# Input products by blocks in chained banks from chunk 7 on, with the sums of w_in made earlier

## The chip, the cores and the metric

The kernel runs on one core of one Trainium2 chip. The metric is the device time of one execution in microseconds (us), the median of several runs. All times below are us unless they are marked ns. The engines are TensorE (PE; PEld is its weight load), VectorE (DVE), ScalarE (ACT), GpSimd (POOL) and SyncE (SP), which here issues the DMAs.

## The reference

Attention with random features for 8 batches, 8 heads, 576 positions and head size 64, followed by a gated feed-forward layer over all 4608 rows:

```python
q_s, k_s = q * scale, k * scale
def phi(x):
    h = x @ omega.T - sum(x * x) / 2
    return exp(h - max(h)) / sqrt(m)          # m = 128 features
kv, z = phi(k_s).T @ v, sum(phi(k_s))
x = (phi(q_s) @ kv) / (phi(q_s) @ z + 1e-6)   # per head; heads side by side: 4608 x 512
h = x @ w_in                                  # 512 x 2048
g = h * tanh(softplus(h))                     # Mish
out = g @ w_out                               # 2048 x 512
```

## The kernel before

The 4608 rows are cut into 18 chunks of 256 rows. For every chunk c the kernel makes the x of its two tiles of 128 rows (attention), an input stage (h = x w_in, Mish, g) and an output stage (g w_out). Operands of the large products are split into two float16 parts, high and low, and a product is three matmuls: low times high, high times low, high times high. The input stage of chunk c stands beside the output stage of chunk c-1: the string `order` in the main loop says for each chunk in what order an input step (`i`) and an output step (`o`) are written. One output step is 12 matmuls of 512 columns into `po`.

The attention runs ahead, as items: one for each batch and pair of heads of k, one for each row tile of q. `pace` says how many items have been given out by a point of a chunk. An item is a generator that runs through the steps of an agenda, one step sixteen times a chunk. An item splits its input (`sk`, `sq`: ScalarE the high part, GpSimd the low), makes the projections (`pk`, `pq`), takes the maximum and subtracts it on VectorE, takes the exponential on ScalarE (`ek`, `eq`), splits again (`kp`, `qn`), and makes `pkv` (keys times values), or transposes by DMA (`qp`) and makes `pn` (queries times `kv`). Values come in as `vf`, with a maximum per batch (`vmx`, then the scale `s_v`), and are split into `vb`. The x of a tile is split into `xs` and transposed by DMA into `xT`. A scheduler orders each engine's instructions from this writing, with costs of its own.

The input stage has two forms:

- `ff_in`, up to chunk 14, is the plain one. A step makes two of the 16 column tiles of h: 24 matmuls of 256 columns into a bank `ph` (pool `ps_h`, two banks). `later(1, mish, ...)` lets ScalarE take Mish out of the bank one step later, and `g_split` splits the result into `g` another step later.
- `ff_in7`, from chunk `SC0` = 15 on, multiplies 2 x 2 blocks by Winograd's scheme with seven products in place of eight. A step is one product: 24 matmuls of 128 columns. Half a chunk's columns (`gr` 0 or 1) takes seven steps. The left operands are blocks of w_in (a11, a12, a22) and four sums of blocks (s1 to s4); the right ones are blocks of x and sums of them (t1 to t4), which `x_sums` makes: four differences on VectorE, four splits and four transposes a chunk in place of two (regions 2 and 3 of x go to tiles `xm`). Each product has a bank `p_...` of its own in `ps_a` (four banks, shared with the attention), and VectorE adds the banks up in the tile `h` (L801).

The sums of w_in are made by `s_make`, in four pieces, written from 16 x (SC0 - 6) + 2 steps behind the start of chunk 2, that is in chunks 11 to 13. VectorE adds and splits, ScalarE copies, and the 16 results go to a scratch in DRAM (`ds`). `ask_sum` loads them back, 256 KB at a time, into a ring of three pairs of slots (`w`), one pair after each product that used a sum.

## Time and profile before

| | |
|---|---|
| median of 3 runs | 964.44 (963.3 to 964.82) |
| the profiled execution | 962.69 |
| its span | 960.8 |
| instructions | 20397 |
| granted TensorE clock, mean | 0.992 |
| busy: PE, PEld, DVE, ACT, POOL | 940.9, 679.3, 624.9, 633.9, 222.7 |
| DMA | 100.25 MB, 147403 packets |

The span runs from the first to the last instruction of one profiled execution; the profiled execution's own time is longer by what lies around the span. A busy time is the sum of an engine's instructions, of which each begins when its inputs are there, so a wait shows as the idle time before an instruction and not in the instruction itself. A matmul's end is modelled, so the length of a group of matmuls is best taken from one group's start to the next one's. A name such as `po<-wo,g` says what an instruction writes and reads, and an arrow behind an idle time names what ended it. "The chain that ended last" is followed back from the last instruction; what stands in it is what set the end.

### The profile page before, as it was taken

The page shows a single profiled execution, that of the slowest core. Times are in us where ns is not written, and L with a number is a line of the kernel's source. Part 1 is how long each engine was busy: PE and PEld are TensorE (multiplying, and loading weights), DVE is VectorE, ACT ScalarE, POOL GpSimd, SP SyncE. Part 2 cuts the span into 40 slices and gives each one's busy share as a digit, 9 for nine tenths or more (in the row PEclk, how much of TensorE's full clock was granted, in tenths as well). Part 3 has the DMA queues.
Part 4 walks back from the last instruction along what each step waited for, and adds up shares of the span by engine and source line. Part 5 has one row for each costly group of instructions (what it writes and reads, how often), then busy time and mean ns, then how long its engine had stood idle before and what let it go on. Part 6 is the DMA issues. An engine that isn't in the chain of part 4 may idle for free. (4 is left out here: it accounts for less than half of the span.)

```text
span 960.8 us, 20397 instructions
## 1 busy us (share of the span) xinstructions
PE 940.9 (98%) x8568; PEld 679.3 (71%) x8568; DVE 624.9 (65%) x1080; ACT 633.9 (66%) x818; POOL 222.7 (23%) x141
## 2 busy tenths in 40 slices
PE   9999988999999999999999999999989999999998
PEld 6788873677677777777777777777756777777663
DVE  5879797587766666656575655788889656643330
ACT  4758875686877877768667775778776866332231
POOL 0000052242432322322133333222231332200000
PEclk9979999999999999999999999999999999999999
DMA  9866314431741346313431253423552145634410
GB/s 287 271 208 208 109 48 94 102 58 61 140 92 37 107 77 119 69 59 75 101 68 53 69 118 66 93 89 68 136 124 73 37 100 115 172 117 131 133 57 33
DMA packets 147403, 100.25 MB, mean 104 GB/s; under 512 B 112112, under 2 KB 124528, under 8 KB 147312
## 3 DMA queue, kind: packets, MB, share of 16 engines
q1 hardware_dynamic: 147312, 98.95, 41.2%
q8 instruction: 67, 1.10, 0.5%
q14 instruction: 24, 0.20, 0.1%
HBM read 58.95 MB, written 13.63 MB: 76 GB/s over the span
## 5 line engine op out<-in xcount | busy, mean ns | idle before, releaser
L858 PE MATMUL po<-wo,g 128*128 128x512 f16 x1632 | 375.2, 380 | 0.0
L689 PE MATMUL ph<-xT,w 128*128 128x256 f16 (+1 forms) x2816 | 344.8, 279 | 0.7 <-ACT xT L72 0.7
L689 PEld LDWEIGHTS <-w 128*128 128x128 f16 x2688 | 261.0, 98 | 47.3 <-issue 0.7
L858 PEld LDWEIGHTS <-g 128*128 128x128 f16 x1632 | 155.1, 98 | 163.9 <-issue 2.2
L83 DVE SCALAR_TENSOR_TENSOR g<-h,us,g 128x1024 f16<-128x1024 f32 (+3 forms) x92 | 120.2, 1316 | 36.8 <-ACT g L72 36.2
L834 ACT ACTIVATE h<-ph,us 128x512 f32<-128x512 f32 (+3 forms) x152 | 83.3, 573 | 77.6 <-PE ph L689 76.8
L81 POOL TENSOR_TENSOR sq<-fq,sq 64x1024 f16<-64x1024 f32 x31 | 69.0, 2227 | 159.1 <-issue 65.2
L81 POOL TENSOR_TENSOR sk<-fk,sk 64x1152 f16<-64x1152 f32 x24 | 60.5, 2520 | 111.5 <-ACT sk L72 86.9
L81 POOL TENSOR_TENSOR xs<-x,xs 128x512 f16<-128x512 f32 (+1 forms) x35 | 44.2, 1264 | 151.9 <-issue 68.0
L72 ACT ACTIVATE g<-h,us 128x1024 f16<-128x1024 f32 (+3 forms) x80 | 72.6, 932 | 1.2
L834 ACT ACT_TABLE_LOAD x55 | 70.6, 1283 | 1.0
L364 ACT ACT_TABLE_LOAD x53 | 68.0, 1283 | 4.2 <-DVE ek L358 3.3
L349 DVE TENSOR_REDUCE mxq<-pq 128x4 f32<-128x512 f32 x72 | 46.8, 682 | 31.7 <-PE pq L340 31.6
L792 PEld LDWEIGHTS <-w 128*128 128x128 f16 x1008 | 58.4, 98 | 5.9
L81 DVE TENSOR_TENSOR qn<-eq,qn 128x1024 f16<-128x1024 f32 x31 | 38.9, 1254 | 36.2 <-ACT qn L72 36.2
L349 DVE TENSOR_REDUCE mxk<-pk 128x4 f32<-128x512 f32 (+1 forms) x96 | 50.1, 548 | 18.0 <-PE pk L340 18.0
L834 ACT ACTIVATE h<-h,us 128x1024 f32<-128x1024 f32 (+2 forms) x16 | 14.7, 933 | 61.9 <-DVE h L801 61.9
L72 ACT ACTIVATE o<-po,us 128x512 f32<-128x512 f32 (+1 forms) x38 | 25.8, 680 | 40.1 <-PE po L858 40.0
L81 DVE TENSOR_TENSOR kp<-ek,kp 128x1152 f16<-128x1152 f32 x24 | 36.4, 1515 | 24.0 <-ACT kp L72 24.0
L364 ACT ACTIVATE eq<-eq,lnt 128x1024 f32<-128x1024 f32 x31 | 35.6, 1148 | 21.2 <-DVE eq L358 21.0
L81 POOL TENSOR_TENSOR vb<-vf,vb 128x640 f16<-128x640 f32 x24 | 39.4, 1641 | 40.6 <-DVE vb L74 28.7
L801 DVE TENSOR_TENSOR h<-p_s,h 128x512 f32<-128x512 f32 x30 | 20.2, 689 | 43.2 <-PE p_s L792 43.2
(140 smaller groups left out, 1156.9 us busy)
## 6 DMA issues: line engine op xcount, KB each, us to landing
w<-ds SPq DMA_DIRECT2D x48, 256.0 KB, 3.4
vf<-in_vL_dram SPq DMA_DIRECT2D x32, 325.0 KB, 3.3
fq<-in_qT_dram SPq DMA_DIRECT2D x36, 256.0 KB, 3.6
out_dram<-o SPq DMA_DIRECT2D x36, 256.0 KB, 2.3
fk<-in_kT_dram SPq DMA_DIRECT2D x24, 256.0 KB, 3.6
raw<-in_w_out_dram SPq DMA_DIRECT2D x5, 1024.0 KB, 8.9
wo<-in_w_in_dram SPq DMA_DIRECT2D x4, 1024.0 KB, 13.2
raw<-in_w_in_dram SPq DMA_DIRECT2D x4, 1024.0 KB, 15.2
```

Of the source, the lines that this page charges most:

```text
L72: act.activation(out, in_, AF.Copy, scale=scale)
L81: eng.tensor_tensor(out=out, in0=in_, in1=hi, op=ALU.subtract)
L83: eng.scalar_tensor_tensor(out=out, in0=in_, scalar=scale, in1=hi, op0=ALU.mult, op1=ALU.subtract)
L349: sub = dve.tensor_reduce(out=mx[:, lo:hi], in_=pp[:, :m, :], axis=AX.X, op=ALU.max, negate=by_act)
L364: last = act.activation(e, e, AF.Exp, bias=lnt)
L689: nc.tensor.matmul(out=ph[:, i, :], lhsT=wi(a, k, f) if c else wi0(k, f), rhs=xT[c][:, y, k, :] if c else xT0()[:, k, :], start=n == 0, st ...
L792: nc.tensor.matmul(out=ph[:, i, :], lhsT=left(gr, op_l, i, a, k), rhs=x_region(c, r)[:, y, k0 + k, :], start=n == 0, stop=n == len(mm) - 1,)
L801: dve.tensor_tensor(out=out, in0=bank, in1=in0, op=ALU.add)
L834: act.activation(h[:, :, lo:hi], ph[:, :, lo:hi], AF.Mish, scale=us[:, 0:1])
L858: nc.tensor.matmul(out=po[i], lhsT=gT[c, gr][:, a, f % FG, i * P:(i + 1) * P], rhs=wo(y, f), start=f == 0 and (a, y) == parts[0], stop=f = ...
```

## The change

`SC0` goes from 15 to 7: chunks 7 to 14 get the block form too, and `s_make` is started at 16 x (7 - 6) + 2 steps behind the start of chunk 2, in chunks 3 to 6. In `ff_in7` the products of a half chunk are chained in banks. The bank `pa` (now of `ps_h`) takes a11, s2, s3 and a22 one on top of the other, and after a11, s2 and s3 ScalarE copies its state into a quarter of h (c11, c12, c22). `pd`, the other bank of `ps_h`, takes s1 and then s4, and VectorE adds it to c22 after s1 and s3 and to c12 after s4. `pb`, of `ps_a`, takes a12, and VectorE adds it to c11. The fourth quarter, c21, is never copied: `mish7` lets ScalarE take Mish straight from `pa`. VectorE makes three adds of 128x512 for a half chunk; ScalarE makes three copies.

The order of the steps is the same but for the last two of each half (`iio` in place of `ioi`), `SUMS` swaps s1 and s3, the tiles `xm` get tags of their own (2 and 1 buffers), the pool of h tiles has 4 buffers in place of 5, the tile `idle` of the first spinning matmuls becomes a part of a weight slot, and from chunk 2 on TensorE's instructions are kept in the order in which they are written (`manual_schedule`).

```diff
-    SC0 = 15
+    SC0 = 7
...
-    idle = const.tile([P, 512], F16, name="idle")
+    idle = slots[NB][:, 0, 0:512]
...
-            x_more[c, r] = sb.tile([P, 2, n, P], F16, tag="vf", name=f"xm{c}_{r}", bufs=5)
+            x_more[c, r] = sb.tile([P, 2, n, P], F16, tag=f"xm{r}", name=f"xm{c}_{r}", bufs=4 - r)
...
-    SUMS = ("s2", "s3", "s1", "s4")
+    SUMS = ("s2", "s1", "s3", "s4")
...
-        def products(gr, op_l, op_r):
+        def products(bank, gr, op_l, op_r, first):
...
-            ph = ps_a.tile([P, FQ, P], F32, tag="a", name=f"p_{op_l}_{c}_{gr}")
             for i in range(FQ):
                 for n, (a, y, k) in enumerate(mm):
                     nc.tensor.matmul(
-                        out=ph[:, i, :], lhsT=left(gr, op_l, i, a, k), rhs=x_region(c, r)[:, y, k0 + k, :],
-                        start=n == 0, stop=n == len(mm) - 1,
+                        out=bank[:, i, :], lhsT=left(gr, op_l, i, a, k), rhs=x_region(c, r)[:, y, k0 + k, :],
+                        start=first and i == 0 and n == 0, stop=n == len(mm) - 1, skip_group_check=True,
                     )
...
-            p1 = products(gr, "a11", "b11")
-            cast(act, c21, p1)
+            pa = bank(ps_h, "h", f"pa{c}_{gr}")
+            products(pa, gr, "a11", "b11", True)
+            cast(act, c11, pa)
             yield
-            add(c11, c21, products(gr, "a12", "b21"))
+            pb = bank(ps_a, "a", f"pb{c}_{gr}")
+            products(pb, gr, "a12", "b21", True)
+            add(c11, pb)
             yield
-            add(c12, c21, products(gr, "s2", "t2"))
+            products(pa, gr, "s2", "t2", False)
+            cast(act, c12, pa)
             yield
-            add(c21, c12, products(gr, "s3", "t3"))
+            pd = bank(ps_h, "h", f"pd{c}_{gr}")
+            products(pd, gr, "s1", "t1", True)
             yield
-            p5 = products(gr, "s1", "t1")
-            add(c22, c21, p5)
-            add(c12, c12, p5)
+            products(pa, gr, "s3", "t3", False)
+            cast(act, c22, pa)
+            add(c22, pd)
             yield
-            add(c12, c12, products(gr, "s4", "b22"))
+            products(pa, gr, "a22", "t4", False)
+            yield
+            products(pd, gr, "s4", "b22", False)
+            add(c12, pd)
+            later(0, mish7, sp, h[1], pa)
+            later(1, g_split, c, gr, 1, sp, h[1])
             later(1, mish, sp, h[0], h[0])
             later(2, g_split, c, gr, 0, sp, h[0])
             yield
-            add(c21, c21, products(gr, "a22", "t4"))
-            later(1, mish, sp, h[1], h[1])
-            later(2, g_split, c, gr, 1, sp, h[1])
-            yield
+
+    def mish7(sp, h, pa):
+
+        for us, lo, hi in sp:
+            if lo < P:
+                e = min(hi, P)
+                act.activation(h[:, :, lo:e], pa[:, :, lo:e], AF.Mish, scale=us[:, 0:1])
+            if hi > P:
+                b = max(lo, P)
+                act.activation(h[:, :, b:hi], h[:, :, b:hi], AF.Mish, scale=us[:, 0:1])
...
-    GB, HB, QB = 4, 5, 1
+    GB, HB, QB = 4, 4, 1
...
+    own = ExitStack()
+    own.enter_context(tc.manual_schedule(engines={mybir.EngineType.PE}))
     for c in range(2, NCH):
         fi, fo = (ff_in if c < SC0 else ff_in7)(c), ff_out(c - 1)
-        order = "io" * 8 if c < SC0 else "iioiioioioi" * 2
+        order = "io" * 8 if c < SC0 else "iioiioioiio" * 2
...
+    own.close()
```

Where the instructions come to stand is shown at three places near the start of chunk 8. First ScalarE before, from the end of chunk 7's second half on (`h` is the tile that takes Mish, `sk` a key item's high part, `eq` and `qn` of a query item):

```order
L834 ACT_TABLE_LOAD
L834 ACTIVATE h_1_1_5353<-ph_1_1_2_5429,us_4234 128x512
L72 ACTIVATE g_1_5195<-h_1_1_5353,us_4234 128x1024
L72 ACTIVATE o_1_5555<-po_1_4945,us_2920 64x512
L72 ACTIVATE o_1_5555<-po_1_4945,us_4234 64x512
L834 ACTIVATE h_0_0_5523<-ph_0_0_0_5524,us_4234 128x512
L834 ACTIVATE h_0_0_5523<-ph_0_0_2_5580,us_4234 128x512
L72 ACTIVATE g_0_5522<-h_0_0_5523,us_4234 128x1024
L72 ACTIVATE sk_1_5799<-fk_1_5714 64x1152
L364 ACT_TABLE_LOAD
L364 ACTIVATE eq_5633<-eq_5633,lnt 128x1024
L72 ACTIVATE qn_5709<-eq_5633 128x1024
```

Now, in the first half of chunk 8:

```order
L72 ACTIVATE h_0_0_5861<-pa_0_5863 128x4x128
L365 ACT_TABLE_LOAD
L365 ACTIVATE eq_5920<-eq_5920,lnt 128x1024
L72 ACTIVATE qn_6032<-eq_5920 128x1024
L72 ACTIVATE h_0_1_5862<-pa_0_5863 128x4x128
L72 ACTIVATE sk_2_6484<-fk_2_6280 64x1152
L847 ACT_TABLE_LOAD
L847 ACTIVATE h_0_1_5862<-h_0_1_5862,us_4364 128x4x128
L365 ACT_TABLE_LOAD
L365 ACTIVATE ek_0_6118<-ek_0_6118,lnt 128x1152
L844 ACT_TABLE_LOAD
L844 ACTIVATE h_0_1_5862<-pa_0_5863,us_4364 128x4x128
```

The first row is the copy to c12, the fifth the copy to c22, the last the Mish that frees `pa`. Between the two copies stand an exponential and a split, and between c22 and the freeing Mish another exponential with its table load.

Second, VectorE in the first half of chunk 8 before:

```order
L358 TENSOR_TENSOR ek_0_5758<-pk_0_0_5760,mxk_0_5759 128x512
L358 TENSOR_TENSOR ek_0_5758<-pk_0_4_5769,mxk_0_5759 128x128
L349 TENSOR_REDUCE mxk_0_5759<-pk_0_5_5772 128x4
L83 SCALAR_TENSOR_TENSOR g_0_5522<-h_0_1_5681,us_4234,g_0_5522 128x1024
L358 TENSOR_TENSOR ek_0_5758<-pk_0_5_5772,mxk_0_5759 128x512
```

Now:

```order
L350 TENSOR_REDUCE mxk_0_6119<-pk_0_0_6120 128x4
L803 TENSOR_TENSOR h_0_1_5862<-pd_0_6002,h_0_1_5862 128x4x128
L359 TENSOR_TENSOR ek_0_6118<-pk_0_0_6120,mxk_0_6119 128x512
L350 TENSOR_REDUCE mxk_0_6119<-pk_0_4_6129 128x1
L350 TENSOR_REDUCE mxk_0_6119<-pk_0_5_6132 128x4
L359 TENSOR_TENSOR ek_0_6118<-pk_0_4_6129,mxk_0_6119 128x128
L359 TENSOR_TENSOR ek_0_6118<-pk_0_5_6132,mxk_0_6119 128x512
L803 TENSOR_TENSOR h_0_0_5861<-pd_0_6002,h_0_0_5861 128x4x128
```

The adds of `pd` to c22 and to c12 (L803) now stand among the maxima and differences of a key item.

Third, SP around the same place, before and then now:

```order
L305 DMA fk_2_5865<-in_kT_dram 64x2x512
L305 DMA fk_2_5865<-in_kT_dram 64x2x64
L481 DMA_TRANSPOSE qp_5550<-qn_5485 128x16x128
L575 DMA_TRANSPOSE xT_4869<-xs_5515 128x8x128
L890 DMA out_dram<-o_1_5555 128x512
```

```order
L540 DMA_TRANSPOSE xm_3_4853<-xs_3_4784 128x4x128
L765 DMA w_81<-ds_0_0_2671 128x2x512
L765 DMA w_82<-ds_0_1_3153 128x2x512
L306 DMA fk_2_6280<-in_kT_dram 64x2x512
L306 DMA fk_2_6280<-in_kT_dram 64x2x64
L540 DMA_TRANSPOSE xT_5024<-xs_1_5851 128x8x128
L540 DMA_TRANSPOSE xm_2_5961<-xs_2_5916 128x8x128
L482 DMA_TRANSPOSE qp_5966<-qn_5855 128x16x128
```

Loads of the sums (`w<-ds`) and two more transposes of x stand ahead of the query transpose (`qp`).

## The prediction

> **What bounds the kernel now.** I read the busy shares first, then busy time chunk by chunk, then the chain that ended last, then the waits of ScalarE and the DMA landings.

> ```profile
> PE 940.9 (98%) x8568; PEld 679.3 (71%) x8568; DVE 624.9 (65%) x1080; ACT 633.9 (66%) x818; POOL 222.7 (23%) x141
> ```

> TensorE is busy for 98% of the span and nothing else passes 71%. A shift of TensorE work should move the end one for one, as long as TensorE does not wait. Next the stretches between the first matmuls of successive output stages; the rows are chunks 3, 4, 5, 6, 8, 12, 13 and 16. Columns: stretch, length, busy PE, PEld, DVE, ACT, POOL, granted clock, DMA share, GB/s.

> ```profile
> 227.98:277.56 49.58, 48.73 (x460) 34.95 (x457) 34.29 (x67) 39.46 (x44) 17.57 (x10) 1.00 0.54 112
> 277.56:326.76 49.20, 49.20 (x475) 35.67 (x473) 30.58 (x62) 38.87 (x52) 16.13 (x9) 1.00 0.22 54
> 326.76:375.46 48.70, 48.70 (x481) 34.98 (x479) 29.55 (x51) 35.65 (x38) 13.62 (x8) 1.00 0.54 99
> 375.46:424.56 49.10, 49.10 (x471) 35.60 (x469) 30.02 (x63) 38.68 (x50) 16.38 (x9) 1.00 0.31 65
> 472.33:521.33 49.00, 49.00 (x469) 35.51 (x467) 29.04 (x54) 30.16 (x31) 12.66 (x7) 1.00 0.26 60
> 667.97:719.93 51.96, 49.48 (x437) 34.29 (x435) 46.11 (x78) 38.77 (x43) 14.96 (x8) 0.97 0.56 126
> 719.93:771.02 51.09, 49.59 (x480) 35.84 (x478) 40.46 (x56) 38.79 (x56) 12.15 (x6) 1.00 0.18 56
> 859.79:899.27 39.48, 39.48 (x436) 28.14 (x433) 14.09 (x18) 11.37 (x13) 0.00 (x0) 1.00 0.38 121
> ```

> A plain chunk takes 49.0 with no idle TensorE. Chunk 16, which already uses the block products, takes 39.48, but has no attention work beside it. Chunks 12 and 13, which hold the sums of w_in, lose 2.48 and 1.50. The chain prices the pieces.

> ```profile
> 810.20 2.62 PE ph L689 x24
> 813.72 2.59 PE po L858 x12
> 882.29 2.68 PE p_s L792 x48
> 887.56 1.34 PE p_s L792 x24
> ```

> Half a plain pair (24 matmuls of 256 columns) is 2.62, one product 1.34, an output group 2.59. Check: 14 x 1.34 + 8 x 2.59 = 39.48, chunk 16 to the digit, so products cost nothing beyond their columns.

> **TensorE work removed.** Chunks 7 to 14 go from 8 x 2.62 = 20.96 to 14 x 1.34 = 18.76: 2.20 per chunk, 17.6 over eight. It is on the path throughout. The attention items are paced by chunk, so their matmuls per chunk stay.

> **Handed-out order of TensorE.** The instruction orders with and without it differ in one place of chunk 3, where two po matmuls stood between two pk groups. Cost 0, at most one pk group (0.7) either way; the rest of the change does not rest on it.

> **The other engines in chunks 7 to 14.**

> ```profile
> L801 DVE TENSOR_TENSOR h<-p_s,h x30: 677/691/692, 823.7 to 932.3; 128x512 f32<-128x512 f32 x30
> L72 ACT ACTIVATE h<-p_a x5: 577/577/597, 840.7 to 918.7; 128x512 f32<-128x512 f32 x5
> L561 DVE TENSOR_TENSOR tt<-x,x x3: 416/416/424, 785.0 to 831.3; 128x256 f32<-128x256 f32 x3
> L834 ACT ACTIVATE h<-ph,us x34: 369/687/690, 425.2 to 618.1; 128x512 f32<-128x512 f32 x32, 128x128 f32<-128x128 f32 x1, 128x384 f32<-128x384 f32 x1
> L764 SPq DMA_DIRECT2D w<-ds x48: 517/518/962, 632.5 to 923.1; - x48
> ```

> VectorE gains per chunk 6 adds (4.1), 4 differences of x (1.7) and about 0.7 of larger splits: 29.0 becomes 35.5 of 46.8, 76%. ScalarE gains 6 copies (3.5), loses about 0.9 of Mish (8 x 0.687 against four 128x512 and two whole tiles), and the order has 14 table loads fewer, 2.2 per chunk at the 1.28 shown below: nearly level. GpSimd gains about 2 for two more remainders of x. SP gains 16 loads (8.3 of issue) and 2 transposes. None becomes the bound by busy time. The smaller pool of h tiles (4 for 5) and the idle tile's new place cost nothing: a half chunk uses two h tiles, and the first writer of that slot comes after the spins. Bound: one wait of 0.7 (an add) either way.

> **The sums of w_in, chunks 3 to 6 instead of 11 to 13.** In the old place, the sums' own instructions (length, DVE, ACT, clock, DMA share, GB/s), TensorE's waits there (total, times, longest), and the output groups ahead of and behind the longest:

> ```profile
> 618.67:771.02 152.35, 48.13 (x55) 10.02 (x16) 0.99 0.34 86
> ...
> PE pk L340 <- DVE x L511: 2.4, 1, 2.4
> PE pkv L445 <- DVE kp L81: 1.9, 2, 1.5
> ...
> 698.32 2.75 PE L858 MATMUL po<-wo,g 128*128 128x512 f16 x12
> 707.08 4.44 PE L858 MATMUL po<-wo,g 128*128 128x512 f16 x12
> ```

> 48.1 of VectorE. It cost a wait of 2.4 and one of 1.5; behind the first, twelve po matmuls took 4.44 where the group ahead took 2.75, with a granted clock of 0.97 over that chunk: 1.7 more. Together 5.6. The new chunks hold 34.3, 30.6, 29.6 and 30.0 of VectorE; with 12 each they come to 42 to 46 of 49, the level of chunks 12 and 13. So I move the 5.6, net 0. Bounds: -5.6 (all hidden) to +5.6 (twice the waits).

> **The waits that the chain of banks adds.** This decides. A plain bank had to be emptied within po + ph + po, 7.8. Now pa takes five products with ScalarE reading between them: after a11 and after s2 the cover is 1.34 + 2.59 = 3.93, after s3 it is 2.59, and Mish must leave pa within s4 + po = 3.93 before the next a11. pd needs c22 from ScalarE, then VectorE's add, within 3.93. Attention matmuls add some 0.7 to each. A copy takes 0.58, so a start up to 2.0 late is free after s3, up to 3.35 elsewhere. How late ScalarE comes today, in its worst quiet place:

> ```profile
> 426.83 1.28 ACT L364 ACT_TABLE_LOAD   x1
> 428.11 2.78 PE L689 MATMUL ph<-xT,w 128*128 128x256 f16 x24
> 429.45 0.82 DVE L278 TENSOR_REDUCE vmx<-vf 128x1 f32<-128x640 f32 x1 [3.68 <-DMA vf<-in_vL_dram]
> 432.49 0.69 DVE L358 TENSOR_TENSOR ek<-pk,mxk 128x512 f32<-128x512 f32 x1
> 433.21 1.26 ACT L364 ACTIVATE ek<-ek,lnt 128x1152 f32<-128x1152 f32 x1 [5.10 <-DVE ek L358]
> 434.54 1.15 ACT L72 ACTIVATE kp<-ek 128x1152 f16<-128x1152 f32 x1
> 435.71 1.28 ACT L834 ACT_TABLE_LOAD   x1
> 437.00 0.69 ACT L834 ACTIVATE h<-ph,us 128x512 f32<-128x512 f32 x1
> ```

> ph ended at 428.11 + 2.78 = 430.89, its Mish began at 437.00, 6.1 late: VectorE stood before a V tile's maximum, ScalarE's exponential behind VectorE, the Mish behind both. TensorE felt nothing. How often, over 340 to 620 (5.7 chunks; total, times, longest):

> ```profile
> ACT h L834 <- PE ph L689: 48.0, 19, 4.5
> ACT ek L364 <- DVE ek L358: 8.9, 4, 5.1
> ACT eq L364 <- DVE eq L358: 5.9, 5, 2.1
> ACT vf L434 <- DVE s_v L124: 5.0, 2, 3.6
> ```

> In 19 cases ScalarE waits for TensorE, as wished. The five eq waits stay under the cover. The six others hold 13.9, and each keeps an exponential and a copy behind it (1.26 + 1.15): 6 x 2.41 = 14.5. Less six covers of 3.35: 8.3 per 5.7 chunks, 11.6 in eight. With the 0.7 of attention in each cover: 4.1, or 5.8 in eight. I take 9, between them. Bounds: 0 (chunk 16) and, with the cover of 2.0 each time, (28.4 - 12.0) x 8 / 5.7 = 23. Behind a product that waits stand, on TensorE, the next output group and the next attention group, and for these VectorE's maxima wait; such a wait empties the other queues too, so I add no second one. pb's place among ps_a's four banks and VectorE's larger share lie inside them.

> [...] Trace: kp ends at 435.69, the load starts at 435.71, Mish at 437.00, so a switch costs 1.28, and Mish leaves pa 1.28 + 0.69 after a22 at best, with 1.96 to spare. [...]

> **Loads and transposes.** Landing times, of qp (stretch 420 to 620) and of the sums (819 to 936):

> ```profile
> DMA to landing us min/median/max: 4.3/4.5/6.3
> ...
> w<-ds SPq DMA_DIRECT2D x42, 256.0 KB, 3.5
> ```

> A slot of the ring is asked for when its product ends and needed 9.2 later at the soonest (s2 to s4: three products and two output groups); two issues of 0.52 and 3.5 leave 4.7. A load that waits for its product holds SP, and the next key loads and qp transposes queue behind it; pn on TensorE waits for qp. Taken at 0, bound 1 per half chunk, 16.

> **Sum.** The profiled execution took 962.69, 1.85 outside its span. 962.69 - 17.6 + 0 + 9 = 954.1. The median of the runs shown, 964.44, is 1.75 above the profiled one: 955.8.

> **Rivals.**

> *The cover holds.* Waits under 4: 946.8 to 951, if the sums cost what they did. For it: the 19 waits of ScalarE for TensorE, and an order that puts most copies ahead of the exponentials. Chance 0.22.

> *Late weights or transposes.* SP waits for buffers that GpSimd frees, and a ring load behind such a wait is late; at 1 per half chunk, without the 9, 962.8. Against: 4.7 of slack. Chance 0.10.

> *Slower: ScalarE's lateness reaches TensorE whole, and the clock drops with it.* Place: a22 behind the copy to c22. A lateness of 6.1 costs 6.1 + 0.58 - 2.59 = 4.1 there, and 1.7 at the lower clock as behind the wait of 2.4: 5.8. More than three of them in eight chunks decide; one per chunk gives 964.4 - 17.6 + 46 = 993, five give 976. Against: such a lateness must meet the shortest cover. Chance 0.12. [...]

> *The sums hurt twice in chunks 3 to 6*: +5.6, 961.4. Chance 0.04.

> [...] The rows above speak against it; chance 0.02. [...]

> **Chances and range.** The forecast has 0.50, own range 951 to 960. Faster by over 0.2% (below 962.5; 0.2% is about what a measurement tells from no change): 0.49 + 0.22 + half of 0.10 + 0.03 = 0.79. Within: 0.08. Slower: 0.13. The range 946 to 967 leaves out the far end of the slower rival (0.11) and a little of the first (0.04).

> **What would show it.** Right: chunks 8 to 10 near 46.8 + 1.1 each, products of 1.34, waits of pa and pd on ACT and DVE of 1 to 4 adding up to about 9, waits of 4 to 6 in chunks 3 to 6 and none left at 706 and 742. Wrong: PE waits on w<-ds or qp, a granted clock under 0.98 in several of chunks 7 to 14, or chunks 7 to 14 at 49.

## The result and the profile after

The changed kernel takes 1006.62 us (median of 4 runs, 1002.34 to 1022.67) against 963.87 for the kernel before: a ratio of 1.042, 95% interval 1.039 to 1.046. It is 4% slower; forecast were 955.8, at most 967. The profiled execution took 1008.6, its span 1006.5.

In some executions, of the kernel before too, the whole takes about 20 us more (in the traces of such executions, `chain_sc15` for one, the granted clock is 0.51 from 15 to 57 us), so single times and medians of few runs below can hold these 20, and stretches are compared from the start of chunk 2 on, behind that time.

The busy shares of the kernel after:

```profile
PE 942.6 (94%) x9720; PEld 688.4 (68%) x9720; DVE 656.0 (65%) x1152; ACT 646.3 (64%) x844; POOL 238.4 (24%) x157
```

TensorE is now idle for 1006.5 - 942.6 = 63.9, before for 19.9: 44.0 more. And its busy time did not fall by the 17.6 of the removed columns; it grew by 1.7. The missing 19.3 are nearly all matmuls at half clock: a mean granted clock of 0.974 over 1006.5, against 0.992 over 960.8, is 18.5 us of lost clock more. So the 45.7 between the spans are 44.0 of idle time and 19.3 of slower matmuls, less the 17.6. No engine took over as the bound: VectorE stands at the same share as before, ScalarE two points lower.

By stretches, first of the kernel before, then after. The rows are chunk 2, chunks 3 to 6 (new place of the sums), 7 to 14 (new block products), and 15 to 17 (block products in both). Columns as in the prediction: length, busy PE, PEld, DVE, ACT, POOL, granted clock, DMA share, GB/s.

```profile
176.54:227.98 51.44, 51.13 (x519) 37.38 (x516) 37.37 (x64) 37.98 (x47) 18.26 (x10) 1.00 0.40 82
227.98:424.56 196.58, 195.73 (x1877) 141.19 (x1875) 124.44 (x240) 152.66 (x181) 63.70 (x36) 1.00 0.40 83
424.56:819.57 395.01, 390.61 (x3712) 280.20 (x3709) 275.10 (x459) 286.55 (x330) 112.09 (x64) 1.00 0.39 87
819.57:936.08 116.51, 116.51 (x1279) 82.54 (x1276) 48.17 (x77) 36.05 (x45) 4.52 (x4) 1.00 0.41 122
```

```profile
179.41:231.29 51.88, 51.13 (x518) 37.46 (x515) 40.20 (x66) 39.47 (x49) 18.29 (x10) 1.00 0.36 85
231.29:444.56 213.27, 201.41 (x1902) 143.57 (x1899) 175.39 (x306) 155.37 (x190) 68.58 (x40) 0.98 0.43 103
444.56:865.51 420.95, 384.92 (x4839) 285.21 (x4837) 265.65 (x486) 284.13 (x324) 123.26 (x76) 0.97 0.65 155
...
865.51:982.02 116.51, 116.51 (x1279) 82.54 (x1276) 35.98 (x57) 47.74 (x65) 4.96 (x4) 1.00 0.48 125
```

Chunks 3 to 6 cost 16.7 more and chunks 7 to 14 cost 25.9 more, where 17.6 less was to come. Chunks 15 to 17 are equal to a hundredth: with chained banks or with four of their own, without attention beside them, the products cost the same. Three single chunks of after, 5, 9 and 13:

```profile
337.39:395.40 58.01, 52.17 (x482) 36.49 (x480) 45.61 (x71) 43.58 (x49) 15.00 (x8) 0.94 0.41 102
...
548.84:609.15 60.31, 50.44 (x634) 37.35 (x632) 34.27 (x58) 38.09 (x45) 17.68 (x9) 0.94 0.59 139
...
767.60:813.82 46.22, 46.22 (x608) 34.91 (x606) 28.74 (x46) 37.39 (x46) 11.55 (x6) 1.00 0.46 135
```

Chunk 13 shows what the block form gives where nothing waits: 46.22, all of it busy, clock 1.00. Chunk 9 holds about the same work (in the plain form of `sums_early`, below, 49.0 against 49.4 for chunk 13) and takes 60.31. Who is waited for? TensorE's waits in after (total, times, longest):

```profile
PE pn L496 <- DMA qp<-qn: 17.8, 12, 3.0
PE pd L792 <- DVE h L803: 8.0, 3, 4.1
PE pn L496 <- DVE ek L359: 5.2, 2, 2.6
PE pkv L446 <- DVE h L803: 4.6, 1, 4.6
PE pk L341 <- DVE x L512: 4.6, 3, 3.5
PE pkv L446 <- DVE kp L81: 3.5, 1, 3.5
PE pa L792 <- ACT h L72: 3.4, 2, 3.2
```

The banks of the chain are 11.4 of it (`pd` 8.0, `pa` 3.4). The wait of 4.6 of `pkv` for an add (L803) is a product's bank too: it waits for the bank that `pb` had in `ps_a`. That makes 16.0. The rest is attention: query transposes (4.4 before, 17.8 now) and products that wait for VectorE. No row names `w<-ds`: the loaded sums came in time. VectorE's own waits, first before, then after:

```profile
DVE vmx L278 <- DMA vf<-in_vL_dram: 27.7, 16, 4.3
...
DVE xs L74 <- DMA xT<-xs: 3.4, 2, 1.7
```

```profile
DVE h L803 <- ACT h L72: 43.5, 10, 9.1
DVE xs L74 <- DMA xT<-xs: 33.6, 10, 6.1
DVE vmx L279 <- DMA vf<-in_vL_dram: 30.4, 14, 4.5
...
DVE xs L74 <- DMA xm<-xs: 16.9, 4, 5.9
```

The largest row, adds that wait for ScalarE's copies, is no cause: 36.3 of its 43.5 lie in chunks 15 to 17, where TensorE never waits, and 7.3 in chunks 7 to 14. But VectorE stands 50.5 before splits of x where it stood 3.4, and 37.8 of that lie in chunks 7 to 14. A split writes a tile `xs`, of which the pool has two; a transpose by DMA empties it. With four splits a chunk in place of two, written one behind the other, the third waits until the first one's transpose has landed, and with it everything behind it in VectorE's order. The waits for V tiles (`vmx`) are as long as before, but something else stands behind them now. The timeline of after in chunks 8 and 9 shows both kinds (start, length, engine and line, operation; in brackets the idle time before it and what ended it):

```profile
539.28 0.29 DVE L74 CAST xs<-x 128x256 f16<-128x256 f32 x1 [5.39 <-DMA xm<-xs]
...
540.76 0.82 DVE L279 TENSOR_REDUCE vmx<-vf 128x1 f32<-128x640 f32 x1 [1.19 <-DMA vf<-in_vL_dram]
541.50 0.68 DVE L803 TENSOR_TENSOR h<-pd,h 128x512 f32<-128x512 f32 x1
...
542.23 1.50 PE L792 MATMUL pd<-xT,w 128*128 128x128 f16 x24 [2.15 <-DVE h L803]
...
570.06 0.82 DVE L279 TENSOR_REDUCE vmx<-vf 128x1 f32<-128x640 f32 x1 [3.30 <-DMA vf<-in_vL_dram]
570.79 0.68 DVE L803 TENSOR_TENSOR h<-pd,h 128x512 f32<-128x512 f32 x1
571.51 0.72 ACT L847 ACTIVATE h<-h,us 128x512 f32<-128x512 f32 x1 [4.35 <-DVE h L803]
571.53 2.72 PE L792 MATMUL pd<-xT,w 128*128 128x128 f16 x24 [4.12 <-DVE h L803]
```

At 539.28 the cast to `xs` ends a wait of 5.39 for a transpose. Behind it stand a V maximum and then the add that empties `pd`; TensorE's s4 product waits 2.15 for that add. At 570.06 the same with a V tile: 3.30 of waiting in VectorE's order, the add at 570.79, ScalarE 4.35 late, TensorE idle for 4.12, and its next product takes 2.72 in place of 1.50, at a granted clock of 0.50 (571.47 to 574.88).

### The profile page after: what moved, and what is told of

Same layout as the page of the kernel before. It is cut to its first block, busy times and chain, and to the rows that moved or that the text cites. A ratio compares the mean times of both kernels' runs of the same rounds, so it can differ in the third digit from the quotient of the medians.

```text
span 1006.5 us, 23109 instructions
## 1 busy us (share of the span) xinstructions
PE 942.6 (94%) x9720; PEld 688.4 (68%) x9720; DVE 656.0 (65%) x1152; ACT 646.3 (64%) x844; POOL 238.4 (24%) x157
## 5 line engine op out<-in xcount | busy, mean ns | idle before, releaser
L876 PE MATMUL po<-wo,g 128*128 128x512 f16 x1632 | 382.1, 386 | 0.0
L792 PEld LDWEIGHTS <-w 128*128 128x128 f16 x3696 | 215.4, 98 | 30.2 <-issue 12.5
L690 PE MATMUL ph<-xT,w 128*128 128x256 f16 (+1 forms) x1280 | 169.0, 289 | 2.3 <-ACT h L852 1.6
L83 DVE SCALAR_TENSOR_TENSOR g<-h,us,g 128x1024 f16<-128x1024 f32 (+3 forms) x92 | 115.5, 1271 | 20.9 <-ACT g L72 20.7
L690 PEld LDWEIGHTS <-w 128*128 128x128 f16 x1152 | 112.8, 99 | 22.5 <-issue 2.9
L81 POOL TENSOR_TENSOR sq<-fq,sq 64x1024 f16<-64x1024 f32 x31 | 67.8, 2190 | 167.6 <-issue 77.6
L81 POOL TENSOR_TENSOR xs<-x,xs 128x512 f16<-128x512 f32 (+1 forms) x43 | 49.0, 1140 | 216.5 <-DVE xs L74 106.8
L72 ACT ACTIVATE h<-pa 128x512 f32<-128x512 f32 x66 | 38.8, 588 | 65.7 <-PE pa L792 65.4
L803 DVE TENSOR_TENSOR h<-pd,h 128x512 f32<-128x512 f32 x44 | 30.2, 686 | 67.7 <-ACT h L72 38.1
L72 ACT ACTIVATE g<-h,us 128x1024 f16<-128x1024 f32 (+3 forms) x80 | 73.1, 931 | 1.4
L792 PE MATMUL pa<-xm,w 128*128 128x128 f16 x1056 | 67.1, 221 | 3.4 <-ACT h L72 3.4
L81 POOL TENSOR_TENSOR sk<-fk,sk 64x1152 f16<-64x1152 f32 x24 | 58.6, 2442 | 41.5 <-ACT sk L72 32.2
L792 PE MATMUL pa<-xT,w 128*128 128x128 f16 x1056 | 66.1, 219 | 0.0
L81 DVE TENSOR_TENSOR qn<-eq,qn 128x1024 f16<-128x1024 f32 x31 | 43.4, 1401 | 26.3 <-ACT qn L72 26.3
L365 ACT ACTIVATE eq<-eq,lnt 128x1024 f32<-128x1024 f32 x31 | 35.6, 1149 | 35.2 <-DVE eq L359 34.8
L81 POOL TENSOR_TENSOR vb<-vf,vb 128x640 f16<-128x640 f32 x24 | 39.7, 1658 | 55.9 <-DVE vb L74 30.1
L496 PE MATMUL pn<-kv,qp 128*128 128x65 f16 (+1 forms) x816 | 29.6, 196 | 23.0 <-DMA qp<-qn 17.8
L72 ACT ACTIVATE o<-po,us 128x512 f32<-128x512 f32 (+1 forms) x38 | 25.8, 680 | 38.3 <-PE po L876 35.4
## 6 DMA issues: line engine op xcount, KB each, us to landing
w<-ds SPq DMA_DIRECT2D x176, 256.0 KB, 3.8
fq<-in_qT_dram SPq DMA_DIRECT2D x36, 256.0 KB, 3.6
out_dram<-o SPq DMA_DIRECT2D x36, 256.0 KB, 2.9
fk<-in_kT_dram SPq DMA_DIRECT2D x24, 256.0 KB, 3.7
```

Of the source, the lines that this page charges most:

```text
L72: act.activation(out, in_, AF.Copy, scale=scale)
L81: eng.tensor_tensor(out=out, in0=in_, in1=hi, op=ALU.subtract)
L83: eng.scalar_tensor_tensor(out=out, in0=in_, scalar=scale, in1=hi, op0=ALU.mult, op1=ALU.subtract)
L365: last = act.activation(e, e, AF.Exp, bias=lnt)
L496: nc.tensor.matmul(out=pn[lo:hi, i, :], lhsT=qp[:, a, h, lo:hi], rhs=kv[b][:, h, y, :], start=n == 0, stop=n == 2,)
L690: nc.tensor.matmul(out=ph[:, i, :], lhsT=wi(a, k, f) if c else wi0(k, f), rhs=xT[c][:, y, k, :] if c else xT0()[:, k, :], start=n == 0, st ...
```

## The experiments

Lengths of the stretches of all kernels, from the starts of the first output groups, of one execution each. Three executions of the kernel after took 1002.34 to 1008.6, so differences of a few us between rows with waits in them say little. "Ideal" is what chunks 7 to 14 would take without a wait: 388.22 (plain form, no sums, all of it busy in `sums_early`) less 17.6 = 370.6.

| kernel | chunk 2 | 3 to 6 | 7 to 14 | 15 to 17 | from chunk 2 |
|---|---|---|---|---|---|
| before | 51.4 | 196.6 | 395.0 | 116.5 | 759.5 |
| after | 51.9 | 213.3 | 421.0 | 116.5 | 802.6 |
| sums_early | 51.4 | 212.5 | 388.2 | 116.5 | 768.6 |
| sums_spread | 58.5 | 208.6 | 421.2 | 116.5 | 804.8 |
| before_sums_spread | 51.4 | 197.6 | 399.2 | 116.5 | 764.7 |
| chain_sc15 | 51.9 | 196.0 | 396.3 | 116.5 | 760.7 |
| unchained7 | 51.9 | 215.0 | 418.2 | 126.2 | 811.3 |
| no_xm | 51.9 | 213.2 | 391.6 | 116.5 | 773.2 |
| no_ring | 51.9 | 210.6 | 406.3 | 116.5 | 785.3 |
| x_spaced | 51.9 | 212.9 | 403.0 | 116.5 | 784.2 |
| x_v_s | 58.8 | 208.1 | 402.7 | 116.5 | 786.0 |
| x_no_vmax | 51.9 | 210.2 | 391.2 | 116.5 | 769.8 |
| blocks_from_13 | 51.9 | 196.3 | 392.9 | 116.5 | 757.6 |
| blocks_from_13_free | 51.9 | 201.9 | 384.8 | 116.5 | 755.1 |

### The sums of w_in alone: sums_early

The kernel before, with its sums at the new place.

```diff
-        at(slot[0] + 16 * (SC0 - 6) + 2 + 11 * i, lambda i=i: start(s_make(i // 2, i % 2)))
+        at(slot[0] + 16 * (7 - 6) + 2 + 11 * i, lambda i=i: start(s_make(i // 2, i % 2)))
```

> The kernel before with one edit: w_in's sums are made in chunks 3 to 6 instead of 11 to 13; blocks still from chunk 15 on. Theory A (the new place of the sums alone costs what chunks 3 to 6 lost, 16.7 over before with the 5.6 of the old place still to come off): about 964 + 16.7 - 5.6 = 975, chunks 3 to 6 about 213 together, with waits of pn and pkv there and three to five drops of the clock. Rival B (the sums move at no net cost, as predicted, and chunks 3 to 6 lost their time to something else of the change): 962 to 966.

Measured: 981.73 (971.79 and 991.68). Chunks 3 to 6 take 212.5, 15.9 more than before and 0.8 less than after; chunks 12 and 13 give back 6.2. Net 9.7. So the sums alone make the loss of chunks 3 to 6 in after, but for 0.8, and the earlier place is much dearer than the later one. The longest of TensorE's waits there, and the output group behind it, of 4.44 where 2.75 is the usual:

```profile
288.83 0.55 PE L495 MATMUL pn<-kv,qp 128*128 128x65 f16 x12 [2.63 <-DVE ek L358]
...
289.21 4.44 PE L858 MATMUL po<-wo,g 128*128 128x512 f16 x12
```

### The chained banks and the handed-out order alone: chain_sc15

```diff
-    SC0 = 7
+    SC0 = 15
```

> The changed kernel with SC0 = 15: chained banks, own tags for xm, four h tiles and the handed-out order, but only three chunks with blocks and the sums in chunks 11 to 13. Theory A (the chained form costs nothing where no attention runs beside it, and the handed-out order is empty): 962 to 966, chunks 15 to 17 at 40.2, 39.5 and 36.8. Rival B (the chain or the handed-out order costs in itself): 970 or more, with waits of pa or pd on ACT in chunks 15 to 17.

Measured: 982.05 (980.34 and 983.77); but chunk 2 starts 19.8 later than in before (196.35 and 176.54), and from there on it takes 760.7 against 759.5. TensorE's handed-out order costs 1.1 at most, and the chain with its copies nothing where attention is over.

### Are the banks the cause in chunks 7 to 14? unchained7

The kernel after with the products' old form: a bank for each in `ps_a`, seven adds on VectorE, no copy but one. The order of the steps and of `SUMS` is the old one too.

```diff
-        def products(bank, gr, op_l, op_r, first):
+        def products(gr, op_l, op_r):
...
+            ph = ps_a.tile([P, FQ, P], F32, tag="a", name=f"p_{op_l}_{c}_{gr}")
...
-            products(pa, gr, "s2", "t2", False)
-            cast(act, c12, pa)
+            add(c12, c21, products(gr, "s2", "t2"))
```

> The changed kernel with the old form of the products: a bank of ps_a for each, added up by VectorE in h (seven adds and one copy for half a chunk), from chunk 7 on; early sums, own tags of xm and the rest as changed. Theory A (the chain of banks lets lateness through, with covers of 2.6 to 3.9, where four banks give more): chunks 7 to 14 under 412. Rival B (the attention's late x, V tiles and queries set the loss, whatever the form): 415 to 430, with waits of p_ banks on VectorE in place of those of pa and pd; VectorE has some 5.5 more a chunk.

Measured: 1016.48, ratio 1.053 (1.051 to 1.055). Its chunks 7 to 14 and what follows:

```profile
444.01:862.25 418.24, 387.46 (x4839) 288.95 (x4837) 303.62 (x546) 263.30 (x273) 121.01 (x74) 0.96 0.64 154
862.25:988.42 126.17, 118.52 (x1279) 83.41 (x1276) 50.72 (x80) 39.74 (x49) 6.08 (x5) 0.97 0.41 114
```

418.2 with four banks and 421.0 with the chain: without the chain as much is lost, so the chain is not what sets the loss. VectorE even works 38 more here (303.62 against 265.65) at the same length, so its load alone does not set it either. What both have in common is the work that feeds them, splits and transposes of x and loads of sums, and adds on VectorE that must empty a bank before TensorE can go on. (The 9.7 more in chunks 15 to 17 are one wait of 7.7 on `qp` in chunk 15, with a granted clock of 0.97 over the stretch.)

### The splits and transposes of x: no_xm and x_spaced

`no_xm` leaves out the splits and transposes of regions 2 and 3 of x (the products read regions 0 and 1 in their place), so its output is another.

```diff
-        for r, src in ((1, xf), (2, tt.rearrange("p a c -> p (a c)")), (3, x0[:, second])):
+        for r, src in ((1, xf),):
```

> The changed kernel without the splits and transposes of x's regions 2 and 3; the products that would read them read regions 0 and 1 instead, so the output is another. VectorE's four differences stay. Theory A (VectorE, held in order at a split that waits for a transpose to free one of the two xs buffers, 50 us of waits after the change and 3.3 before, is what starves TensorE): chunks 7 to 14 fall from 421 to 395 or less, about 980 in all. Rival B (the loads of the sums on SP's queue are the cause): about 1000 to 1006, chunks 7 to 14 still over 412. Rival C (VectorE's waits for V tiles): the same as B here.

Measured: 978.19, ratio 1.014 (1.011 to 1.017), and chunks 7 to 14 at 391.6: 29.3 of the 50.3 above the ideal are gone. VectorE's waits at `xs` for a DMA are gone altogether. This run takes away GpSimd's remainders and SP's transposes for these splits as well; the next one doesn't.

`x_spaced` keeps the work and only writes the splits further apart, so that a transpose lands before its buffer is needed:

```diff
         for r, src in ((1, xf), (2, tt.rearrange("p a c -> p (a c)")), (3, x0[:, second])):
+            yield 2 if r > 1 else 0
             yield from x_send(nth, c, r, src)
```

> The changed kernel with two steps more before the splits of x's regions 2 and 3, so that their xs buffers are free when VectorE comes to them; all work stays. Compared from chunk 2 on. Theory A (VectorE held at the splits is what costs): VectorE's waits for transposes of x fall from 50 to under 15 and chunks 7 to 14 from 421 to about 395, 975 to 982 in all, close to the run without these splits. Rival B (it was the work of the splits itself: GpSimd's remainders, SP's transposes, DMA share): the waits move, and chunks 7 to 14 stay over 410.

Measured: 996.07 (985.62 and 1006.51), chunks 7 to 14 at 403.0, between the two expectations. Two rows of VectorE's waits:

```profile
DVE xs L74 <- DMA xm<-xs: 15.1, 6, 9.0
DVE xs L74 <- DMA xT<-xs: 12.4, 5, 6.3
```

27.5 of waits in place of 50.5, and 18.0 of time; the lower of the two runs is 16.7 below the lowest of after. With no other change than two steps of distance, this shows that when VectorE comes to the two `xs` buffers is worth 18 us. A third buffer, which would test the size of the pool itself, was not tried.

### The loads of the sums: no_ring

All but the first loads into the ring are left out (6 of 176), so that products use stale sums.

```diff
-        if n < len(uses):
+        if n < min(3, len(uses)):
```

> The changed kernel without the reloads of the ring: the first three pairs of sums are loaded once and every later product reads what lies there, so the output is another; 170 of 176 loads are left out. Theory A (VectorE's splits that wait for xs buffers): little changes, 995 to 1006, since transposes still wait for GpSimd; a gain of some us through earlier transposes. Rival B (SP's queue, held by loads that wait for their product, and the DMA engines' share): chunks 7 to 14 at 395 or less, about 980. Rival C: V tiles come earlier with a freer SP, the vmx waits fall from 30 under 20, some 5 to 10 us.

Measured: 998.63 (989.46 and 1007.79), chunks 7 to 14 at 406.3: 14.6 less. No product ever waited for a sum, so the cost is indirect. SP's waits in after show a way (times in which it stood before an instruction, and for whom; 40.6 of the two rows lie in chunks 7 to 14):

```profile
SPq L765 <- PE pa L792: 55.9, 26, 7.9
...
SPq L765 <- PE pd L792: 26.5, 19, 6.5
```

A load of a sum stands in SP's order until its product has ended, and key loads and transposes stand behind it. But without the loads the DMA share in these chunks falls too, from 0.65 to 0.37, and this run does not tell SP's order from the DMA engines' load. The causes overlap, since the transposes that VectorE waits for are issued by SP: 29.3 and 14.6 can't be added.

### The V tiles: x_v_s and x_no_vmax

Both start from `x_spaced`. `x_v_s` writes the maxima of V later (and has the sums of `sums_spread`, below):

```diff
-        yield 3 if b else 1
+        yield (3 if b < 4 else 7) if b else 1
```

> Three edits together on the changed kernel: splits of x spaced, the pieces of the sums 18 steps apart from chunk 2 on, and the maximum of V tiles written four steps later from batch 4 on, so that VectorE does not stand before a V tile that has not landed. Theory (three in-order holds on VectorE make most of the loss): chunks 7 to 14 at 380 to 390, chunks 2 to 6 at 255 or less, about 960. Rival (the chain of banks lets any lateness through, so other holds take their place): over 975.

Measured: 991.12, ratio 1.028 (1.024 to 1.032). Chunks 7 to 14 take 402.7 as without it, and VectorE waits for V tiles for 26.5 in 13 cases (28.4 in 13 in `x_spaced`). Writing the maxima later moved them nowhere that helped: a miss. Why the wait went along was not tried. `x_no_vmax` takes the maxima away: from batch 4 on a constant 4.0 stands in their place, so the scale of V no longer depends on a load.

```diff
+            if b < 4:
                 dve.tensor_reduce(
...
+            else:
+                dve.memset(mx[:, hp:hp + 1], 4.0)
```

> The kernel with spaced splits of x, and without the maxima of V tiles from batch 4 on: a constant 4.0 stands in their place, so VectorE no longer waits there for a V tile to land; scales differ, the rest stays. Theory A (VectorE held before a V tile, 28 us of waits in 13, is the second hold): vmx waits of batches 4 on go, chunks 7 to 14 fall from 403 to 385 to 392, chunk 9 from 58 to under 52. Rival B (the tile itself comes late, SP's queue being held, and its next reader waits instead): chunks 7 to 14 at 398 or more, and ScalarE or pkv waits in its place.

Measured: 979.79 (974.12 and 985.47), chunks 7 to 14 at 391.2, 11.8 less than `x_spaced`; chunk 9 fell from 58.1 to 51.8. A wait that TensorE hardly felt in the kernel before (27.7 on VectorE) costs up to 12 here; the maxima's own work, 0.82 each, went with the wait, and the two were not separated. What is left, 391.2 against 370.6, is mostly attention's own (waits of the whole run):

```profile
PE pn L499 <- DMA qp<-qn: 16.9, 12, 3.2
PE pn L499 <- DVE ek L362: 6.9, 2, 4.2
PE pa L796 <- ACT h L72: 3.2, 1, 3.2
```

The granted clock was 0.99 over chunks 7 to 14 (0.97 in after). Which of SP, VectorE or ScalarE holds each wait was not taken apart further.

### A better place for the sums: sums_spread and before_sums_spread

The pieces 18 steps apart from chunk 2 on, in the kernel after; and 18 steps apart in chunks 6 to 9, in the kernel before.

```diff
-        at(slot[0] + 16 * (SC0 - 6) + 2 + 11 * i, lambda i=i: start(s_make(i // 2, i % 2)))
+        at(slot[0] + 2 + 18 * i, lambda i=i: start(s_make(i // 2, i % 2)))
```

> The changed kernel with the four pieces of w_in's sums started from chunk 2 on, 18 steps apart in place of 11, so that VectorE has at most one piece a chunk. Theory A (chunks 3 to 5 lose their 17 because the pieces are packed): chunks 2 to 6 together fall from 265 to about 255, 997 or less in all. Rival B (each piece costs its wait wherever it stands, through GpSimd's and VectorE's clash and the banks of pk and pn): chunks 2 to 6 stay at 262 to 268.

> The kernel before with one edit: the four pieces of w_in's sums 18 steps apart from chunk 6 on, in place of 11 apart from chunk 11 on. Theory (one piece a chunk is free where the attention is well ahead, as chunks 4 and 5 of the spread run showed; packed pieces cost 6.2 in chunks 12 and 13): 957 to 960, chunks 6 to 14 without waits. Rival (a piece costs wherever it stands): 962 to 966.

Measured: `sums_spread` 1017.91 (1008.53 and 1027.29), its chunks 2 to 6 at 267.0, as the rival had it; `before_sums_spread` 983.21 (968.6 to 987.49), from chunk 2 on 764.7 against 759.5, 5.2 more and worse than its rival. No gain in either. Chunks 2 to 5 of `sums_spread`, a piece in each:

```profile
196.01:254.49 58.48, 53.92 (x517) 38.19 (x515) 52.23 (x78) 40.62 (x53) 17.57 (x10) 0.94 0.39 95
254.49:314.44 59.95, 50.85 (x459) 35.45 (x457) 50.24 (x81) 40.77 (x46) 17.23 (x10) 0.97 0.50 114
314.44:363.64 49.20, 49.20 (x476) 35.68 (x473) 40.96 (x73) 37.29 (x50) 16.12 (x9) 1.00 0.23 69
363.64:412.34 48.70, 48.70 (x482) 34.97 (x479) 42.59 (x59) 37.62 (x43) 12.75 (x7) 1.00 0.44 107
```

A piece is some 12 of VectorE's work (48.1 in four). It cost 7.0 and 10.4 in chunks 2 and 3, and in chunks 4 and 5 nothing at all: 49.20 and 48.70 are the lengths of before. In `before_sums_spread` chunks 3, 7 and 9 have TensorE waits of 1.8 (for VectorE), 3.0 and 3.0 (on `qp`); 7 and 9 held a piece, 3 did not. The place of a piece decides its cost; whether by what stands behind it in VectorE's order was not taken apart.

### A version that is faster: blocks_from_13 and blocks_from_13_free

Blocks where attention is nearly over, with the splits spaced and the pieces in chunks 6 to 9:

```diff
-    SC0 = 7
+    SC0 = 13
...
+            yield 2 if r > 1 else 0
...
-        at(slot[0] + 16 * (SC0 - 6) + 2 + 11 * i, lambda i=i: start(s_make(i // 2, i % 2)))
+        at(slot[0] + 66 + 18 * i, lambda i=i: start(s_make(i // 2, i % 2)))
```

> The changed kernel with SC0 = 13, spaced splits of x and the sums 18 steps apart from chunk 6 on. Theory (chunks 13 and 14 keep the gain of 2.2 each since the attention is nearly done there, the chain is free, the spread sums are free): 953 to 957. Rival (chunks 13 and 14 lose it to the same holds): 958 to 964.

Measured: 962.49 (median of 10) against 965.71 for before, ratio 0.9975 (0.9964 to 0.9985): a quarter of a per cent faster, less than expected. Chunks 13 and 14 gained what they should (47.2 and 46.6; 49.4 and 48.6 in `sums_early`, plain form without sums). Chunks 7 and 9 lost to pieces of the sums:

```profile
425.17:476.43 51.26, 48.11 (x447) 34.09 (x445) 38.67 (x62) 37.51 (x45) 15.73 (x8) 1.00 0.41 110
525.43:579.67 54.24, 50.98 (x488) 35.64 (x486) 40.07 (x64) 39.96 (x47) 16.76 (x9) 0.97 0.34 88
```

The last run put the pieces where they had been free:

```diff
-        at(slot[0] + 66 + 18 * i, lambda i=i: start(s_make(i // 2, i % 2)))
+        at(slot[0] + (38, 56, 66, 102)[i], lambda i=i: start(s_make(i // 2, i % 2)))
```

> The kernel of blocks_from_13 with one thing changed: the four pieces of the sums of w_in start 38, 56, 66 and 102 steps behind the start of chunk 2 (in chunks 4, 5, 6 and 8) instead of 66, 84, 102 and 120 (chunks 6, 7, 8 and 9). A piece in each of these four places left its chunk at the length it has without one in an earlier run: 49.2 and 48.7 for chunks 4 and 5 in sums_spread, 49.1 and 49.0 for chunks 6 and 8 in blocks_from_13. Chunks 7 and 9, which took 51.26 and 54.24 in blocks_from_13, took 47.77 and 49.02 without a piece in sums_early. Theory (a piece costs by what stands at its place in VectorE's order, and by nothing else): chunks 7 and 9 come back to 47.8 and 49.0, from chunk 2 on 757.6 - 3.5 - 5.2 = 749, the median near 954, between 952 and 957. Rival (the four pieces' work has to be paid somewhere, because VectorE's queue carries the lateness on): another chunk takes the loss, from chunk 2 on 755 to 760, the median 960 to 964.

Measured: 958.75 (median of 6) against 965.6, ratio 0.992 (0.990 to 0.995), the fastest kernel of this study. The time lies between the two expectations, the 755.1 at the lower end of the rival's. Chunks 6, 7 and 9:

```profile
377.27:430.62 53.35, 50.79 (x471) 36.29 (x469) 41.28 (x85) 42.10 (x55) 16.95 (x10) 0.97 0.40 101
430.62:478.39 47.77, 47.77 (x447) 34.25 (x445) 30.12 (x50) 38.10 (x43) 15.39 (x9) 1.00 0.46 103
527.39:577.08 49.69, 49.20 (x488) 35.21 (x486) 27.71 (x51) 38.77 (x43) 18.07 (x9) 1.00 0.31 75
```

Chunks 7 and 9 came back to 47.8 and 49.7, as the theory of places had it. But chunk 6, free with one piece, lost 4.3 with two pieces ten steps apart: a wait of 2.56 on `qp` at 385.20 and, behind it, an output group of 3.71 at 386.52 where 2.75 is the usual, with a granted clock of 0.97 over the chunk. That place was free for one piece, not for two.

## Why the prediction was wrong

**TensorE work removed, -17.6: right.** Chunks 13 and 14 of `blocks_from_13` are 2.2 and 1.9 shorter than the plain ones of `sums_early`, against 2.20 forecast. The gain is there in after too; it is under the losses.

**Handed-out order, 0: right,** within the 1.1 of `chain_sc15`.

**The other engines, no bound: right by the sums, and the wrong question.** Their busy shares hardly moved. VectorE's 76% were compared with the chunk's length; what cost time was the order in which VectorE stands still.

**The sums, net 0: wrong by 9.7.** The step "with 12 each they come to 42 to 46 of 49, the level of chunks 12 and 13. So I move the 5.6, net 0" failed. The pieces stood mostly in three chunks, not four (46.6, 47.4 and 45.6 of VectorE in chunks 3 to 5 of after, 35.7 in chunk 6), not far above that level, and yet the cost was 15.9 in place of 6.2, beyond the bound of twice the waits. Equal load is not equal cost: in `blocks_from_13` chunks 7 and 9, with 38.7 and 40.1 of VectorE, lost 3.5 and 5.2; in `sums_spread` chunks 4 and 5, with 41.0 and 42.6, lost nothing.

**Loads and transposes, "taken at 0": this step failed most.** The landing of the loads was checked (right: no wait on `w<-ds`), and the rival "late weights or transposes" named the `qp` waits that came (17.8 in 12 cases). But the two buffers of `xs`, with four splits a chunk instead of two, were not looked at; the splits were priced only by their length. `no_xm` gives back 29.3 of 50.3, `x_spaced` 18.0 without taking work away, and `no_ring` 14.6, where the bound was 16 for all of it.

**The waits added by the chain, +9: the size within its bounds, the reason not.** TensorE's direct waits for product banks are 16.0, of which `pa` and `pd` have 11.4. The forecast's chain came once: at 565.91 a22 waited 3.15 behind a copy, the copy behind an exponential, and this behind a V tile on VectorE (4.07). The other 12.6, of `pd` and `pb`, come from adds that stand on VectorE itself behind `xs` and V tiles (4.61 for `xs` before the wait at 625.83); the forecast looked for lateness on ScalarE. So the size is partly luck, and `unchained7` loses as much without a chain. The sentence "such a wait empties the other queues too, so I add no second one" was wrong: the same holds delay keys and queries, and their waits came on top.

**The clock, left out of the sum** but for the 1.7 inside the sums' 5.6. 19.3 of the 63 lost (45.7 + 17.6) are slower matmuls; the trace records eleven windows of 3.4 at half clock more than in before, at 1.7 each 18.8. Only the slower rival had this term for the added waits. Its price per event, 5.8, and its time at one event per chunk, 993, were near what chunks 7 to 14 did (50.3 lost, 6.3 per chunk); its place, a22 behind the copy to c22, held for one wait (the 3.15, without a drop of the clock right behind it), so the nearness is luck. With the rival of the sums on top it would have been 993 + 5.6 = 998.6.

**The switch of ScalarE's table, 1.28: right.** In after a load starts at 548.39 and the exponential behind it at 549.68, 1.29 later; the 46 loads at that line (L365) take 1.28 each.

Of the signs of "wrong" all came but a wait on `w<-ds`: waits on `qp`, a clock under 0.98 in six of chunks 7 to 14, and chunks 7 to 14 at 46.2 to 60.3, 52.6 on average.

## What to carry to other kernels

A wait that is hidden today is no reserve that can be given out twice: VectorE stood 27.7 before V tiles at hardly any cost, until an add that TensorE needs within 4 us was put behind it. When a change puts a short-deadline step into an in-order queue, list what in that queue waits for DMAs, and count the buffers of each pool the added steps go through, before adding up busy times. And price a long wait expected on TensorE with half clock behind it: in after, 10 of the 12 waits of 2.37 us or more were followed by it, at 1.7 us for a window.

## Of the hardware

```profile
561.23:564.64 3.41, 1.53 (x8) 0.59 (x6) 2.29 (x6) 1.74 (x3) 1.23 (x1) 1.00 0.96 300
564.64:568.06 3.42, 1.50 (x24) 1.38 (x24) 1.37 (x2) 2.50 (x3) 0.18 (x1) 1.00 1.04 218
...
687.53:690.94 3.41, 1.21 (x32) 1.10 (x33) 3.41 (x7) 2.73 (x5) 1.95 (x1) 1.00 0.12 35
690.94:694.35 3.41, 3.41 (x10) 1.21 (x9) 3.19 (x6) 1.97 (x4) 0.62 (x2) 0.50 0.32 77
```

**VectorE beside GpSimd.** In `sums_early` an add of 128x512 took 2.85 while GpSimd ran its remainder, and 0.69 a little later without it:

```profile
284.13 2.69 POOL L81 TENSOR_TENSOR sk<-fk,sk 64x1152 f16<-64x1152 f32 x1
284.52 2.85 DVE L724 TENSOR_TENSOR s<-s,w 128x512 f32<-128x512 f32 x1
...
292.00 0.69 DVE L724 TENSOR_TENSOR s<-s 128x512 f32<-128x512 f32 x1
```

So an add of the sums took four times as long beside GpSimd as one without it. In after it is the same: of the 40 adds of the sums (L725), the 31 with no GpSimd instruction beside them took 0.66 to 0.69, and the three that began within 0.4 behind the start of a GpSimd remainder (287.57, 302.03 and 362.23) took 2.85, 2.86 and 2.61. This may be part of why a piece's place matters. At this place it is: the add ends at 287.37, a maximum and a difference follow it on VectorE, and TensorE's wait of 2.63 above ends at 288.83, behind that difference. For the other places it was not taken apart.
